# Attention of block 2 computed with channels as rows, its k times v moved into the written-out order

## The chip, the cores and the metric
One core of one Trainium2 chip runs the kernel. The metric is the device time of a run in microseconds (us), as the median of three runs. Engines are called PE (TensorE: matrix products), PEld (its weight loads), ACT (ScalarE), DVE (VectorE), POOL (GpSimd) and SP (SyncE, which here only issues DMAs).

## What is computed
Linear attention without softmax over 8 batches of 576 tokens with 8 heads of 64 channels, an RMS norm per head, and then two feed-forward layers over the 4608 tokens.

```python
kv = np.einsum('bhsd,bhse->bhde', k, v)
out = np.einsum('bhsd,bhde->bhse', q, kv)
rms = np.sqrt(np.mean(out * out, axis=-1, keepdims=True) + 1e-06)
x = (out / rms * g_norm)                       # as rows of 8 * 64 = 512
h = np.maximum(np.maximum(x @ w1, x @ w2), x @ w3)
y = h @ w_out                                  # 512 -> 768 -> 512
xn = y / np.sqrt(np.mean(y * y, -1, keepdims=True) + 1e-6) * rms_g
g = xn @ w_gate
result = (g * sigmoid(g) * (xn @ w_val)) @ w_out2   # 512 -> 1536 -> 512
```

## The kernel before
**Tiles and stages.** The 4608 tokens are cut in nine blocks of 512 (TB), counted 0 to 8. The activations of a block are kept with channels as rows, `X[t]`, as two tiles of fp32r whose sum is the value (a high and a low part). The ordinary product of the layers, mm3, is three fp32r products of 128x512 (high by high, high by low, low by high); twelve of them, four blocks of channels c, make one column block of a projection. P1.3.2 in the order below is such a group for block 1, column block 3, weight matrix 2. Plain fp32 products, which need no split, are used where operands are small.

**Attention.** For a batch b, kv_part(b, 0 to 4) multiplies k by v head by head: 40 products of 64x64 into one PSUM tile pk. kv_copy(b) takes pk out. From batch 2 on, kv_split writes the two parts of it to kvr: two ACT copies (L349), one for each half of the partitions, and two DVE subtractions (L351). Batches 0 to 2 are also copied by ACT (L366, L367) to kvbd, a matrix of 128x128 blocks on the diagonal, in fp32.
- Blocks 0 to 2 go token by token (128 tokens each, token_steps): po multiplies q by kvbd (L407), ACT squares, DVE sums over the heads, POOL takes the power -0.5, DVE scales (xn, L384), PE transposes (pt, L435), and ACT and DVE write the two parts of X.
- Blocks 3 to 8 go with channels as rows (wide_block): q and kv are both split and multiplied by mm3, ACT keeps the product and its square, DVE sums the squares in pieces, two products with the matrix fold (halves) complete the sums, POOL takes the power over 32 columns, and the factors are brought to their places through DRAM (spread, respread to the tile fr). The output then needs no transposes.

**What sets the order.** The kernel writes its own order; each engine runs its instructions as they come. Up to column block 3 of block 1 the string ORDER is read word by word: `ld:x` issues a load on SP, `P` a group of 12 products, `kv2.0` a part of k times v, `kc2` kv_copy, `s1`, `s2`, `h`, `hsI`, `hsL` the steps of the maximum and its split, and the letters A U X S H B I L the eight steps in which the weights, which come as 64-bit floats, are converted (A, H, B, L on DVE, U, X, S, I on ACT); Uo4 is step U for block 4 of w_out. After the string the rest runs in slots: `at(n, fn)` plans fn for the n-th next slot, and tick() runs the slot's functions between two groups of products. In do_p(t, j, mid) three groups of 12 follow each other with a slot between them.

**Buffers.** All weights, raw loads, q, kv and split tiles share one pool of 37 buffers of 4 KB per partition, up. A tile takes a buffer that is free or about to be, and its first writer then waits for the last user of the buffer. PSUM has two pools of four buffers.

In the kernel before, block 2 and batch 2 stand at the seam: its loads `ld:q4 ld:kv2` are issued late in ORDER, its k times v is in the first slot after ORDER (kv_do(0, 2)), its four tokens are planned at slots 1, 3, 5 and 7, and q block 5 is loaded in slot 2. `build_fold()` stands after ORDER.

```python
kv_do(0, 2)
for m in range(NS):
    token(1 + 2 * m, 2 * NS + m)
at(2, lambda: load_q(5))
at(3, lambda: new_x(2))
kv_load_at(6, 3)
kv_do(13, 3)
do_p(0, J1 - 1, pumped)
```

Of the kernel before, what the change touches and what calls it, by code (L numbers as in the profile page):

```python
# [20 lines left out]
P = 128  # L21
# [4 lines left out]
TB = 512  # L26
# [1 line left out]
NS = TB // P  # L28
KC = DM // P
NP = H // 2  # L30
WIDE = 3
WIDE_KV = WIDE * 512 // 576
J1, J2 = F1 // P, F2 // P
EPS = 1e-6
TOP = float(np.array(0x47F00000, dtype=np.uint32).view(np.float32))
# [15 lines left out]
hsL0.2 Bw32 Uo2 P1.1.0 Lw31 Iw32 Xo2 Lw32 So2 Ho2 P1.1.1 s11.1 Bo2 Io2 Lo2 P1.1.2 s21.1 ld:w50 P0.3.0 h1.1  # L51
hsI1.1 hsL1.1 Aw40 Uw40 ld:w51 P0.3.1 s10.3 Xw40 Sw40 Hw40 ld:w52 Aw41 Uw41 P0.3.2 Bw40 Xw41 s20.3 Iw40 Sw41
Lw40 ld:o4 Aw42 Uw42 Hw41 O0.2 Xw42 h0.3 Bw41 Sw42 hsI0.3 Hw42 Iw41 Ao3 hsL0.3 Bw42 Uo3 P1.2.0 Lw41 Iw42 Xo3
Lw42 So3 Ho3 P1.2.1 s11.2 Bo3 Io3 Lo3 P1.2.2 s21.2 ld:o5 P0.4.0 h1.2 hsI1.2 hsL1.2 Aw50 Uw50 P0.4.1 s10.4 Xw50
Sw50 Hw50 Aw51 Uw51 P0.4.2 Bw50 Xw51 s20.4 Iw50 Sw51 Lw50 Aw52 Uw52 Hw51 O0.3 Xw52 ld:q4 ld:kv2 h0.4 Bw51 Sw52
hsI0.4 Hw52 Iw51 Ao4 hsL0.4 Bw52 Uo4 P1.3.0 Lw51 Iw52 Xo4 Lw52 So4 Ho4 P1.3.1 s11.3 Bo4 Io4 Lo4 P1.3.2 s21.3
h1.3 hsI1.3 hsL1.3 Ao5 Uo5 Xo5 So5 Ho5 Bo5 Io5 Lo5
"""

# [2 lines left out]
def tile_kernel(ctx: ExitStack, tc, qT, k, v, kvt0, kvt1, w1, w2, w3, wo, wg, wv, wo2, out):  # L62
# [29 lines left out]
    def f32(ap):  # L92
        return ap.bitcast(F32)
# [260 lines left out]

    def kv_copy(b):
        pk = PK.pop(b)
        if b >= WIDE_KV:
            kv_split(pk, b)
        if b > WIDE_KV:
            del KV[b]  # L360
            kvbd.clear()
            kvb.clear()
            return
        m = kvb[b % 2]
        n = NP // 2 if b == 0 else NP
        nc.scalar.activation(m[:D, :n, 0:D], pk[:D, :n], AF.Copy)  # L366
        nc.scalar.activation(m[D:, :n, D:], pk[D:, :n], AF.Copy)  # L367
        if b == 0:
            pk = PK.pop("odd")
            nc.vector.tensor_copy(m[:D, n:, 0:D], pk[:D, n:])  # L370
            nc.vector.tensor_copy(m[D:, n:, D:], pk[D:, n:])
        kvbd[b] = m
        del KV[b]
# [77 lines left out]
    def cut_of(i):  # L451
        return slice(i % NS * P, (i % NS + 1) * P)

    def token(n, i):

        st = token_steps(i)
        for m, names in ((0, ("po", "sq")), (1, ("ss", "pw")), (3, ("xn",)), (4, ("pt", "hi")), (5, ("lo",))):
            for name in names:
                at(n + m, st[name])

    def wide_block(t, s):

        st = {}
        nb = TB // 32

        def split(m):
            if m == 0:
                st["y"] = xp.tile([P, KC, TB], F32, tag="x", name="y")
                st["hi"] = xp.tile([P, KC, TB], F32R, tag="x", name="qh")
                st["part"] = hp.tile([P, KC, nb], F32, tag="part", name="part")  # L470
            for c in range(2):
                nc.scalar.activation(st["hi"][:, 2 * m + c], Q[2 * t + m][:, c], AF.Copy)

        def rest(m):
            q = Q.pop(2 * t + m)
            lo = st["lo", m] = unit([P, 2, TB], F32R, "ql")
            for c in range(2):
                nc.vector.tensor_tensor(lo[:, c], q[:, c], f32(st["hi"][:, 2 * m + c]), ALU.subtract)

        def po(c):  # L480
            hi, lo = st["hi"][:, c], st["lo", c // 2][:, c % 2]
            o = psum([P, TB], "po")
            b = t * TB // S
            n = min(TB, (b + 1) * S - t * TB)
            for w, f in ((kvr[b], slice(0, n)), (kvr.get(b + 1), slice(n, TB))):
                if f.start < f.stop:
                    mm3(o[:, f], w[:, 0, c], w[:, 1, c], hi[:, f], lo[:, f], True, True)
            if c % 2:
                del st["lo", c // 2]
            if c + 1 == KC:  # L490
                del st["hi"]
            nc.scalar.activation(st["y"][:, c], o, AF.Copy)
            sq = st["sq", c] = tmp("sq")
            nc.scalar.activation(sq, o, AF.Square)

        def part(c):
            sq = st.pop(("sq", c)).rearrange("p (j b) -> p b j", b=nb)
            nc.vector.tensor_reduce(st["part"][:, c], sq, AX.X, ALU.add, apply_transpose=True)

        def halves():  # L500
            st["ss"] = psum([P, 2, nb], "hs")
            part = st["part"]
            for m in range(2):
                nc.tensor.matmul(st["ss"], fold[:, m], part[:, 2 * m:2 * m + 2], start=m == 0, stop=m == 1)

        def factor():
            rs = st["rs"] = hp.tile([P, 2, nb], F32, tag="rs", name="rs")
            nc.vector.tensor_scalar(rs, st["ss"], 1.0 / D, EPS, ALU.mult, ALU.add)
            flat = rs.rearrange("p q b -> p (q b)")
            nc.gpsimd.tensor_tensor(flat, flat, mhalf.to_broadcast([P, 2 * nb]), ALU.pow)  # L510

        def spread():
            nc.scalar.dma_start(hr_d[t].rearrange("q (r f) -> (q r) f", f=2 * nb), st["rs"].rearrange("p c b -> p (c b)"))

        def respread():
            for n in range(2):
                if n == 0:
                    st["f"] = xp.tile([P, KC, TB], F32, tag="x", name="fr")
                nc.scalar.dma_start(
                    st["f"][n * D:(n + 1) * D].rearrange("p c f -> p (c f)"), hr_d[t][n:n + 1].to_broadcast([D, KC * TB])  # L520
                )

        def xn(c):
            x = st["x", c] = tmp("xn")
            f = st["f"].rearrange("p (m c) f -> p m (c f)", m=2)[:, c // 2]
            f = f.rearrange("p (j c b) -> p c j b", c=2, b=nb)[:, c % 2]
            xv, yv = (a.rearrange("p (j b) -> p j b", b=nb) for a in (x, st["y"][:, c]))
            nc.vector.scalar_tensor_tensor(xv, yv, gc, f, ALU.mult, ALU.mult)

        def hi(c):  # L530
            if c == 0:
                new_x(t)
            nc.scalar.activation(X[t][0][:, c], st["x", c], AF.Copy)
# [376 lines left out]
    def at(n, fn):  # L910
        plan.setdefault(n_slot[0] + n, []).append(fn)
# [251 lines left out]
    with tc.manual_schedule():  # L1163
# [43 lines left out]
                nc.gpsimd.tensor_tensor(hs[:, 1], mx.pop((t, j)), f32(hs[:, 0]), ALU.subtract)  # L1207

        for word in ORDER.split():
            if word == "gc":  # L1210
                nc.scalar.activation(gcb, first_tail[0][:, DM:DM + 1 + KC], AF.Copy)
                continue
            m = re.match("[a-z]+|[A-Z]", word)
            kind, rest = m.group(), word[m.end():]
            if word.startswith("hs"):
                kind, rest = word[:3], word[3:]
            elif word[:2] in ("s1", "s2"):
                kind, rest = word[:2], word[2:]
            if kind in "AUXSHBIL":
                weight_step(kind, weight_key(rest))  # L1220
                continue
            if kind == "ld":
                load_word(rest[1:])
                continue
            n = [int(x) for x in rest.split(".")]
            if kind == "kv":
                kv_part(*n)
            elif kind == "kc":
                kv_copy(n[0])
            elif kind == "busy":  # L1230
                busy(n[0])
            elif kind == "P":
                up_word(*n)
            elif kind == "O":
                do_o(1, *n, J1)
            elif kind in ("s1", "s2", "h", "hsI", "hsL"):
                max_word(kind, *n)
            else:
                tok[n[0]][kind]()
        build_fold()  # L1240

        def pumped():
            tick()
# [5 lines left out]
        def kv_do(n, b):  # L1249
            at(n, lambda: do_kv(b))  # L1250

        kv_do(0, 2)
        for m in range(NS):
            token(1 + 2 * m, 2 * NS + m)
        at(2, lambda: load_q(5))
        at(3, lambda: new_x(2))
        kv_load_at = lambda n, b: at(n, lambda: load_kv(b))
        kv_load_at(6, 3)
        kv_do(13, 3)
# [8 lines left out]
        wait += [Prep(i, jp) for jp in range(J2 // 2) for i in range(3)]  # L1268
        for j in range(J1 - 1):
            if j in (1, 3):  # L1270
                load_q(2 * WIDE + j // 2)
            do_o(1, 1, j, J1)
            slot()

# [134 lines left out]
```

## Time and profile before

| | before |
|---|---|
| median of 3 runs | 1454.26 us (1454.23 to 1454.78) |
| the profiled execution | 1454.48 us, span in the trace 1452.7 us |
| PE busy | 1445.7 us of the span, 7106 products |
| DVE busy | 925.0 us |
| ACT busy | 637.6 us |
| POOL busy | 433.5 us |

A timeline gives start, duration, engine, line, operation, tiles, shapes and count, and in brackets how long the engine was idle before and what ended it. Products overlap: what one costs is the distance from its start to the next one's, not its duration. A plain fp32 product has two records on PE, so eight records of L407 are four products.

### The profile page before, as it was taken

What the parts mean: (1) busy time and instruction counts of PE and PEld (TensorE: products, weight loads), DVE (VectorE), ACT (ScalarE), POOL (GpSimd) and SP (SyncE); (2) the same over time, 40 slices, a digit from 0 to 9 for tenths busy, and PEclk for the clock granted to TensorE, in tenths of its full rate; (3) what the DMA queues carried; (4) which work ended last, traced back from release to release, by engine and by line L of the source; (5) the groups of instructions that cost most, each with busy time, mean ns of one, the idle gap of its engine ahead of it and who ended that gap; (6) DMA issues with size and microseconds to landing.
All of it is one profiled execution on the core that took longest, in us unless ns stands there. A gap on an engine that the chain in (4) does not pass through costs nothing.

```text
span 1452.7 us, 19796 instructions
## 1 busy us (share of the span) xinstructions
PE 1445.7 (100%) x7106; PEld 1204.4 (83%) x7106; DVE 925.0 (64%) x1401; ACT 637.6 (44%) x1136; POOL 433.5 (30%) x295
## 2 busy tenths in 40 slices
PE   9999999999999999999999999999999999999999
PEld 8888888888888888888888888888888888888887
DVE  6854477786768695962446475664675655754756
ACT  6863355454545564622224333343243442433422
POOL 3212231313131313121332252441334422532423
PEclk9999999999999999999999999999999999999999
DMA  9432357575757565769669464784666843784542
GB/s 366 156 94 81 95 182 268 189 259 186 281 194 261 188 248 184 275 251 393 232 217 349 158 248 187 284 302 183 231 243 252 329 175 132 297 310 175 192 177 102
DMA packets 109426, 324.13 MB, mean 223 GB/s; under 512 B 13264, under 2 KB 13520, under 8 KB 108560
## 3 DMA queue, kind: packets, MB, share of 16 engines
q1 hardware_dynamic: 95840, 296.14, 55.5%
q10 hardware_dynamic: 13488, 26.73, 5.8%
q8 instruction: 56, 0.92, 0.3%
q14 instruction: 42, 0.34, 0.1%
HBM read 249.30 MB, written 73.52 MB: 222 GB/s over the span
## 4 chain that ended last, share of the span: by engine, by line
PE 99%; DVE 0%; issue 0%; ACT 0%; POOL 0%; POOLq 0%
PE ua L922 18%; PE p L558 10%; PE p L559 10%; PE p L560 10%; PE ub L922 9%; PE da L922 9%; PE db L922 4%; PE uc L922 4%; PE acc L558 4%; PE acc L559 4%; PE acc L560 4%; PE dc L922 2%; PE pk L334 1%; PE pg L558 1%; PE pg L560 1%; PE pv L560 1%
## 5 line engine op out<-in xcount | busy, mean ns | idle before, releaser
L558 PE MATMUL p<-x,w 128*128 128x512 f32 (+1 forms) x656 | 255.9, 390 | 0.0
L560 PE MATMUL p<-x,w 128*128 128x512 f32 (+1 forms) x656 | 253.7, 387 | 0.0
L559 PE MATMUL p<-x,w 128*128 128x512 f32 (+1 forms) x656 | 253.7, 387 | 0.0
L922 PE MATMUL ua<-xo,w 128*128 128x512 f32 x864 | 213.4, 389 | 0.0
L922 PEld LDWEIGHTS ua<-xo,w 128*128 128x128 f32 x864 | 162.2, 188 | 33.7
L577 POOL TENSOR_TENSOR ho<-sl,ho 128x512 fp32r<-128x512 f32 x72 | 98.2, 1370 | 302.1 <-ACT ho L576 274.2
L577 POOL TENSOR_TENSOR hs<-h,hs 128x512 fp32r<-128x512 f32 x45 | 67.3, 1496 | 393.2 <-ACT hs L576 384.0
L577 POOL TENSOR_TENSOR ho<-t,ho 128x512 fp32r<-128x512 f32 x96 | 123.9, 1295 | 134.0 <-ACT ho L576 81.2
L922 PE MATMUL ub<-xo,w 128*128 128x512 f32 x576 | 146.1, 389 | 0.0
L560 PEld LDWEIGHTS p<-x,w 128*128 128x128 f32 x656 | 123.2, 188 | 25.2
L558 PEld LDWEIGHTS p<-x,w 128*128 128x128 f32 x656 | 123.3, 188 | 24.7
L559 PEld LDWEIGHTS p<-x,w 128*128 128x128 f32 x656 | 123.3, 188 | 24.0
L922 PEld LDWEIGHTS ub<-xo,w 128*128 128x128 f32 x576 | 108.1, 188 | 22.4
L1004 ACT ACTIVATE s<-ua 128x512 f32<-128x512 f32 x96 | 57.3, 597 | 138.6 <-PE ua L922 138.6
L922 PE MATMUL da<-ho,wd 128*128 128x512 f32 x432 | 105.7, 389 | 0.0
L576 ACT ACTIVATE ho<-t 128x512 fp32r<-128x512 f32 x96 | 59.4, 627 | 99.9 <-DVE t L753 98.9
L922 PEld LDWEIGHTS da<-ho,wd 128*128 128x128 f32 x432 | 81.1, 188 | 16.8
L576 ACT ACTIVATE hs<-h 128x512 fp32r<-128x512 f32 x45 | 28.4, 632 | 135.3 <-DVE h L593 126.8
L952 DVE TENSOR_TENSOR c<-uc,s 128x512 f32<-128x512 f32 x48 | 33.1, 690 | 83.8 <-PE uc L922 83.8
L558 PE MATMUL acc<-hs,w 128*128 128x512 f32 x216 | 85.1, 394 | 0.0
L560 PE MATMUL acc<-hs,w 128*128 128x512 f32 x216 | 84.3, 390 | 0.0
L559 PE MATMUL acc<-hs,w 128*128 128x512 f32 x216 | 84.0, 389 | 0.0
(173 smaller groups left out, 2692.7 us busy)
## 6 DMA issues: line engine op xcount, KB each, us to landing
w<-wd SPq DMA_DIRECT2D x180, 512.0 KB, 7.3
wd<-ws SPq DMA_DIRECT2D x72, 512.0 KB, 3.3
wd<-wd SPq DMA_DIRECT2D x72, 512.0 KB, 7.0
wq<-wd SPq DMA_DIRECT2D x72, 256.0 KB, 7.8
xo<-td SPq DMA_DIRECT2D x32, 512.0 KB, 9.4
q<-in_qT SPq DMA_DIRECT2D x18, 512.0 KB, 5.6
raw<-in_w SPq DMA_DIRECT2D x18, 512.0 KB, 10.3
raw<-in_wo SPq DMA_DIRECT2D x18, 512.0 KB, 6.2
```

Of the source, the lines that this page charges most:

```text
L334: nc.tensor.matmul(pk[h * D:(h + 1) * D, hp, :], kk, vv, start=(c == 0 and hp in ((0, NP // 2) if b == 0 else (0,))), stop=(c == 4), skip_ ...
L558: nc.tensor.matmul(o, ah, bh, start=first, stop=False)
L559: nc.tensor.matmul(o, ah, bl, start=False, stop=False)
L560: nc.tensor.matmul(o, al, bh, start=False, stop=last)
L576: nc.scalar.activation(hs[:, 0], h, AF.Copy)
L577: nc.gpsimd.tensor_tensor(hs[:, 1], h, f32(hs[:, 0]), ALU.subtract)
L922: nc.tensor.matmul(o, aa, bb, start=first and q == 0, stop=last and q == 2, skip_group_check=True)
L952: nc.vector.tensor_tensor(t, p, s, ALU.add)
L1004: nc.scalar.activation(t, p, AF.Copy)
```

## The change
Block 2 becomes the first wide block (WIDE is 2), with a chain of its own: no split of q and kv, but four plain fp32 products of q (as columns) with kvbd, cut at the border between batches 1 and 2 (plain); the sums, the power and the way through DRAM are those of the other wide blocks, with the three DMAs on SP's queue in place of ACT's. The loads of q blocks 4 and 5 and of batch 2 move ahead of P0.4.0, the fold copies ahead of P1.2.2, and batch 2's k times v, its copies and the start of the wide block (the word wide, which runs one slot) ahead of P1.3.2. The token steps of block 2 are gone.

```diff
-WIDE = 3
-WIDE_KV = WIDE * 512 // 576
+WIDE = 2
+SPLIT_KV = (WIDE + 1) * TB // S
...
-Lw42 So3 Ho3 P1.2.1 s11.2 Bo3 Io3 Lo3 P1.2.2 s21.2 ld:o5 P0.4.0 h1.2 hsI1.2 hsL1.2 Aw50 Uw50 P0.4.1 s10.4 Xw50
-Sw50 Hw50 Aw51 Uw51 P0.4.2 Bw50 Xw51 s20.4 Iw50 Sw51 Lw50 Aw52 Uw52 Hw51 O0.3 Xw52 ld:q4 ld:kv2 h0.4 Bw51 Sw52
-hsI0.4 Hw52 Iw51 Ao4 hsL0.4 Bw52 Uo4 P1.3.0 Lw51 Iw52 Xo4 Lw52 So4 Ho4 P1.3.1 s11.3 Bo4 Io4 Lo4 P1.3.2 s21.3
+Lw42 So3 Ho3 P1.2.1 s11.2 Bo3 Io3 Lo3 fold P1.2.2 s21.2 ld:o5 ld:q4 ld:q5 ld:kv2 P0.4.0 h1.2 hsI1.2 hsL1.2 Aw50 Uw50 P0.4.1 s10.4 Xw50
+Sw50 Hw50 Aw51 Uw51 P0.4.2 Bw50 Xw51 s20.4 Iw50 Sw51 Lw50 Aw52 Uw52 Hw51 O0.3 Xw52 h0.4 Bw51 Sw52
+hsI0.4 Hw52 Iw51 Ao4 hsL0.4 Bw52 Uo4 P1.3.0 Lw51 Iw52 Xo4 Lw52 So4 Ho4 P1.3.1 s11.3 Bo4 Io4 Lo4 kv2.0 kv2.1 kv2.2 kv2.3 kv2.4 kc2 wide P1.3.2 s21.3
...
+        first = t == WIDE
+        queue = nc.sync if first else nc.scalar
...
+        def plain(c):
+            if c == 0:
+                st["y"] = []
+                st["part"] = hp.tile([P, KC, nb], F32, tag="part", name="part")
+            if c % 2 == 0:
+                y = unit([P, 2, TB], F32, "y")
+                st["y"] += [y[:, 0], y[:, 1]]
+            q = Q[2 * t + c // 2][:, c % 2]
+            o = psum([P, TB], "po")
+            b = t * TB // S
+            n = min(TB, (b + 1) * S - t * TB)
+            nc.tensor.matmul(o[:, :n], kvbd[b][:, c, :], q[:, :n], start=True, stop=True)
+            if n < TB:
+                nc.tensor.matmul(o[:, n:], kvbd[b + 1][:, c, :], q[:, n:], start=True, stop=True)
+            if c % 2:
+                del Q[2 * t + c // 2]
+            keep(c, o)
...
+        if first:
+            for c in range(KC):
+                at(s + c // 2, lambda c=c: plain(c))
+                at(s + 1 + c // 2, lambda c=c: part(c))
+                at(s + 11 + c // 2, lambda c=c: xn(c))
+                at(s + 12 + c // 2, lambda c=c: hi(c))
+                at(s + 13 + c // 2, lambda c=c: lo(c))
+            for m, fn in ((4, halves), (5, factor), (7, spread), (7, respread)):
+                at(s + m, fn)
+            return
...
+            if word == "wide":
+                wide_block(WIDE, 0)
+                tick()
+                continue
+            if word == "fold":
+                build_fold()
+                continue
...
-        build_fold()
...
-        kv_do(0, 2)
-        for m in range(NS):
-            token(1 + 2 * m, 2 * NS + m)
-        at(2, lambda: load_q(5))
-        at(3, lambda: new_x(2))
```

PE around batch 2's k times v, before. The first row ends the first group of do_p(0, 5), the last rows begin its second; a name in brackets is a semaphore that the instruction waits for (DMAHW0 to 7 are those of the loads).

```order
L560 MATMUL p_1291<-x,w 128x512
L334 MATMUL pk<-kv 64x64 [waits DMAHW7_49,DMAHW2_49,Activation_49]
L334 MATMUL pk<-kv 64x64 x15
L334 MATMUL pk<-kv 64x64 [waits DMAHW3_49,DMAHW0_49]
L334 MATMUL pk<-kv 64x64 x7
L334 MATMUL pk<-kv 64x64 [waits DMAHW4_49,DMAHW1_49]
L334 MATMUL pk<-kv 64x64 x15
L558 MATMUL p_1355<-x,w 128x512 [waits DVE_49]
L559 MATMUL p_1355<-x,w 128x512
```

PE around the same products now. The row before them ends P1.3.1; L487 and L489 are the two products of plain for c=0 and c=1, and L585 begins P1.3.2 (L585 to L587 are mm3, L558 to L560 before).

```order
L587 MATMUL p<-x,w 128x512
L334 MATMUL pk<-kv 64x64 [waits DMAHW3_49,DMAHW0_49,DVE_49]
L334 MATMUL pk<-kv 64x64 x15
L334 MATMUL pk<-kv 64x64 [waits DMAHW4_49,DMAHW1_49]
L334 MATMUL pk<-kv 64x64 x7
L334 MATMUL pk<-kv 64x64 [waits DMAHW5_49,DMAHW2_49]
L334 MATMUL pk<-kv 64x64 x15
L487 MATMUL po<-q,kvbd 128x128 [waits DMAHW6_49,DVE_49]
L489 MATMUL po<-q,kvbd 128x384 [waits Activation_49]
L487 MATMUL po<-q,kvbd 128x128
L489 MATMUL po<-q,kvbd 128x384
L585 MATMUL p<-x,w 128x512 [waits PE_49]
```

The k times v has moved ahead of P1.3.2, and products with q stand directly behind it, the second of them with a wait for ACT.

ACT over the conversion of o4 and batch 2's copies, before. L138, L118, L140 and L150 are the steps U, X, S and I; the first row is Uo4, the second Iw52, the sixth Io4; L1197 is s11.3, L1204 hsI1.3, and after it come the same four steps for o5.

```order
L138 ACTIVATE wt<-raw 128x512 [waits DMAHW4_49,PE_49,Pool_49]
L150 ACTIVATE w<-wt 128x512 [waits DVE_49,Activation_49]
L118 ACTIVATE wt<-wt 128x512
L140 ACTIVATE wt<-wt 128x512 [waits Activation_49]
L1197 ACTIVATE s_1231<-p 128x512 [waits PE_49]
L150 ACTIVATE w<-wt 128x512 [waits DVE_49]
L1204 ACTIVATE hs<-h 128x512 [waits DVE_49]
...
L585 ACTIVATE s_1304<-p_1291 128x512
L349 ACTIVATE kvr<-pk 64x4x64 [waits DMAHW2_49,PE_49,Pool_49]
L349 ACTIVATE kvr<-pk 64x4x64
L366 ACTIVATE kvbd<-pk 64x4x64 [waits DVE_49]
L367 ACTIVATE kvbd<-pk 64x4x64
```

The same steps now, from Uo4 (the first row) to the copies of the first wide product; L1224 is s11.3.

```order
L138 ACTIVATE wt<-raw 128x512 [waits DMAHW4_49,DMAHW0_49,PE_49]
L150 ACTIVATE w<-wt 128x512 [waits DMAHW3_49,DVE_49]
L118 ACTIVATE wt<-wt 128x512 [waits Activation_49]
L140 ACTIVATE wt<-wt 128x512 [waits Activation_49]
L1224 ACTIVATE s_1257<-p 128x512
L150 ACTIVATE w<-wt 128x512 [waits DMAHW1_49,DMAHW4_49,DVE_49,PE_49]
L349 ACTIVATE kvr<-pk 64x4x64 [waits PE_49,Pool_49]
L349 ACTIVATE kvr<-pk 64x4x64
L366 ACTIVATE kvbd<-pk 64x4x64 [waits DVE_49]
L367 ACTIVATE kvbd<-pk 64x4x64
L509 ACTIVATE y<-po 128x512 [waits PE_49]
L511 ACTIVATE sq<-po 128x512
```

The split and the copies of batch 2 have moved directly behind Io4, and Uo4 has DMAHW0 and another place of PE in its wait.

## Rows read from the trace of the kernel before
**Rows 1.** The page: busy time by engine, granted clock by slice, shares of the chain
```profile
PE 1445.7 (100%) x7106; PEld 1204.4 (83%) x7106; DVE 925.0 (64%) x1401; ACT 637.6 (44%) x1136; POOL 433.5 (30%) x295
...
PEclk9999999999999999999999999999999999999999
...
PE 99%; DVE 0%; issue 0%; ACT 0%; POOL 0%; POOLq 0%
```

**Rows 2.** Timeline of PE, 118 to 125 us: start, duration, what
```profile
118.46 2.55 PE L334 MATMUL pk<-kv 128*64 128x64 f32 x80
120.94 0.50 PE L558 MATMUL p<-x,w 128*128 128x512 f32 x1
121.27 0.39 PE L559 MATMUL p<-x,w 128*128 128x512 f32 x1
121.50 0.40 PE L560 MATMUL p<-x,w 128*128 128x512 f32 x1
...
123.79 1.05 PE L407 MATMUL po<-kvbd,q 128*128 128x128 f32 x8
124.60 0.48 PE L558 MATMUL p<-x,w 128*128 128x512 f32 x1
124.92 0.40 PE L559 MATMUL p<-x,w 128*128 128x512 f32 x1
```

**Rows 3.** Timeline of PE: transposes ahead of L407, and ahead of ordinary products
```profile
141.93 0.60 PE L435 MATMUL pt<-ident,xn 128*128 128x128 f32 x4
142.37 1.06 PE L407 MATMUL po<-kvbd,q 128*128 128x128 f32 x8
...
161.72 0.60 PE L435 MATMUL pt<-ident,xn 128*128 128x128 f32 x4
162.08 0.48 PE L558 MATMUL acc<-hs,w 128*128 128x512 f32 x1
```

**Rows 4.** Timeline of PE: the halves of block 3
```profile
192.52 0.53 PE L504 MATMUL hs<-part,fold 128*128 128x32 f32 x4
192.88 0.48 PE L558 MATMUL acc<-hs,w 128*128 128x512 f32 x1
193.20 0.39 PE L559 MATMUL acc<-hs,w 128*128 128x512 f32 x1
```

**Rows 5.** Timeline of ACT: Uo4, So4, s11.3 and Io4
```profile
107.73 0.67 ACT L138 ACTIVATE wt<-raw 128x512 int32<-128x512 uint32 x1 [0.48 <-issue]
...
110.43 0.63 ACT L140 ACTIVATE wt<-wt 128x512 f32<-128x512 f32 x1
110.97 0.58 ACT L1197 ACTIVATE s<-p 128x512 f32<-128x512 f32 x1
112.28 0.63 ACT L150 ACTIVATE w<-wt 128x512 fp32r<-128x512 f32 x1 [0.73 <-DVE wt L146]
```

**Rows 6.** Timeline of DVE: Lo4
```profile
112.94 0.69 DVE L152 TENSOR_TENSOR w<-wt,w 128x512 fp32r<-128x512 f32 x1 [0.70 <-ACT w L150]
```

**Rows 7.** Timeline of ACT: split and copies of batch 2
```profile
121.52 0.75 ACT L349 ACTIVATE kvr<-pk 64x256 fp32r<-64x256 f32 x2
125.14 0.38 ACT L366 ACTIVATE kvbd<-pk 64x256 f32<-64x256 f32 x1 [2.86 <-DVE kvr L351]
125.53 0.38 ACT L367 ACTIVATE kvbd<-pk 64x256 f32<-64x256 f32 x1
```

**Rows 8.** Timeline of DVE: low parts of batch 2's split
```profile
124.24 0.86 DVE L351 TENSOR_TENSOR kvr<-pk,kvr 64x256 fp32r<-64x256 f32 x2
```

**Rows 9.** Timeline of PE at the start: warming products
```profile
1.36 5.49 PE L307 MATMUL busy<-ident 128*128 128x128 f32 x24 [1.36 <-POOL ident masks.py:199]
...
8.05 2.05 PE L307 MATMUL busy<-ident 128*128 128x128 f32 x16
```

**Rows 10.** Power of the wide blocks (ns min/median/max); DMA issues with median us to landing
```profile
L510 POOL TENSOR_TENSOR rs<-rs,mhalf x6: 5556/5728/6031, 196.8 to 556.2; 128x32 f32<-128x32 f32 x6
...
fr<-hr ACTq DMA_DIRECT2D x12, 512.0 KB, 6.3
```

More of the change, by code (lines that the diff above doesn't have):

```diff
@@ L356, in kv_copy @@
         pk = PK.pop(b)
-        if b >= WIDE_KV:
+        if b >= SPLIT_KV:
             kv_split(pk, b)
-        if b > WIDE_KV:
+        if b > SPLIT_KV:
             del KV[b]
@@ L452, in cut_of @@
         return slice(i % NS * P, (i % NS + 1) * P)
[L454 to L459, printed above, removed]
     def wide_block(t, s):
@@ L464, in wide_block @@
         nb = TB // 32
+        first = t == WIDE
+        queue = nc.sync if first else nc.scalar
         def split(m):
             if m == 0:
-                st["y"] = xp.tile([P, KC, TB], F32, tag="x", name="y")
+                y = xp.tile([P, KC, TB], F32, tag="x", name="y")
+                st["y"] = [y[:, c] for c in range(KC)]
                 st["hi"] = xp.tile([P, KC, TB], F32R, tag="x", name="qh")
@@ L491, in po, with keep @@
                 del st["hi"]
-            nc.scalar.activation(st["y"][:, c], o, AF.Copy)
+            keep(c, o)
+        def keep(c, o):
+            nc.scalar.activation(st["y"][c], o, AF.Copy)
             sq = st["sq", c] = tmp("sq")
@@ L512, in spread @@
         def spread():
-            nc.scalar.dma_start(hr_d[t].rearrange("q (r f) -> (q r) f", f=2 * nb), st["rs"].rearrange("p c b -> p (c b)"))
+            queue.dma_start(hr_d[t].rearrange("q (r f) -> (q r) f", f=2 * nb), st["rs"].rearrange("p c b -> p (c b)"))
         def respread():
@@ L518, in respread @@
                     st["f"] = xp.tile([P, KC, TB], F32, tag="x", name="fr")
-                nc.scalar.dma_start(
+                queue.dma_start(
                     st["f"][n * D:(n + 1) * D].rearrange("p c f -> p (c f)"), hr_d[t][n:n + 1].to_broadcast([D, KC * TB])
@@ L526, in xn @@
             f = f.rearrange("p (j c b) -> p c j b", c=2, b=nb)[:, c % 2]
-            xv, yv = (a.rearrange("p (j b) -> p j b", b=nb) for a in (x, st["y"][:, c]))
+            xv, yv = (a.rearrange("p (j b) -> p j b", b=nb) for a in (x, st["y"][c]))
             nc.vector.scalar_tensor_tensor(xv, yv, gc, f, ALU.mult, ALU.mult)
@@ L1270, in tile_kernel @@
             if j in (1, 3):
-                load_q(2 * WIDE + j // 2)
+                load_q(2 * WIDE + 2 + j // 2)
             do_o(1, 1, j, J1)
```

## The prediction
> **What bounds the kernel now.** I read the head of the page first: TensorE (PE) is busy for 1445.7 of 1452.7 us, and the chain that ended last is 99% PE [rows 1]. So whatever PE no longer issues comes off the end, and whatever PE newly waits for is put on it; the other engines count only where PE waits for them. The profiled execution took 1454.48 us, 0.2 more than the median of 1454.26; the terms below are differences, and I set them on the median.
>
> **What PE gets rid of, and what it gets.** PE's timeline shows prices as distances between starts. Ordinary 128x512 products follow each other every 0.23 us; the second product after a block of plain fp32 ones starts 0.32 to 0.33 after the first, so a change back costs 0.09 to 0.10 [rows 2].
> - Removed: four token steps of q times kv (L407). One is 8 records, from 123.79 to 124.60, 0.81 us, and 0.09 for the change back: 4 x 0.90 = 3.60 [rows 2].
> - Removed: four groups of transposes (L435). One that stands right ahead of an L407 block costs 0.44 (141.93 to 142.37) with no change back of its own, one ahead of ordinary products 0.36 and 0.09 [rows 3]. I take 0.44 for each of the four: 1.76.
> - Added: four plain fp32 products of 512 columns, each cut in two at column 128. That is the same number of columns as in four L407 blocks. At L407's price per column they cost 4 x 0.81 = 3.24; the bound from above is four passes, each at the 0.23 of an ordinary product: 4 x 4 x 0.23 = 3.7. I take 3.24, since L407 is the same kind of product. They come in two groups, and the first follows k times v directly, whose change back (0.10) it shares: one change more, 0.09, so 3.33.
> - Added: the two products that sum the squares (halves). Their twins at L504 take 0.36 and 0.09 for the change back [rows 4]: 0.45.
> - k times v of batch 2 only moves: 2.48 us before and after [rows 2].
>
> The sum for PE is -5.36 + 3.33 + 0.45 = **-1.58 us**, and -1.1 with the dearer bound. That is all that the change can gain.
>
> **Where the new place makes PE wait.** In the order of before, batch 2's k times v is followed by 12 ordinary products and then by a token that still reads batch 1; the first product with the new matrix comes after four such groups of 12 (12 x 0.227 = 2.72 us each) and that token. In the changed order the word wide issues its first two products at once: kv, kc2, c=0 on 128 columns of batch 1, and then c=0 on 384 columns with the matrix that kc2 has just begun to write. PE takes its work in order, so P1.3.2 and everything behind it is queued behind that wait. The row of L489 names ACT as what it waits for: the copies L366 and L367. L366 in turn waits for DVE's L351, in the order of before as well.
>
> How late is that copy? On ACT, ahead of the split and the copies, stands the conversion of the weight o4, from Uo4 to Io4. In the order of before Uo4 ran at 107.73, beside P1.3.0 [rows 5]. In the changed one its row waits for DMAHW0, on which the first k load of batch 2 lands, and for PE: by the value in the built program, for the 16th of batch 2's 40 products. The pool of 37 buffers is that short once two q blocks and five kv buffers are loaded ahead: the working buffer of o4 is one that batch 2's rows leave. So a conversion that used to run beside products begins only when batch 2's own products run. Let t0 be the start of the first of these:
> - 16 of 40 products are issued at 0.4 x 2.48 = 0.99, and I allow 0.25 for the last one to end and be seen (an estimate): Uo4 starts at t0 + 1.25.
> - From Uo4 to the start of Io4 the trace has the same instructions in the same order: 107.73 to 112.28, 4.55 us [rows 5]. Io4 starts at t0 + 5.80.
> - L349 follows on ACT 0.54 later, the distance at which ACT starts work that waits for nothing (110.43 to 110.97), and takes 0.75 for its two halves [rows 5, 7]: t0 + 7.1. On DVE, Lo4 starts 0.66 after Io4 does (112.94) and is nearly through by then [rows 6].
> - A handover takes 0.03 there (112.28 + 0.63 to 112.94); L351 on DVE takes 0.86 [rows 6, 8]: t0 + 8.0. L366 and L367 take 0.77 [rows 7]: t0 + 8.8, and PE goes on at about t0 + 8.85.
> - Without the wait PE would be there at t0 + 2.48 + 0.2 = t0 + 2.68.
>
> The stall is **6.2 us**, with bounds half a microsecond to either side for the six handovers of the chain. Nothing hides it, as PE takes no work past it. The sum is -1.58 + 6.2 = **+4.6 us**.
>
> **What the clock may add.** The granted clock is at its upper level (2.4 GHz) in every slice of the page [rows 1]. But the first 24 warming products take 5.49 us, 0.229 each, and 16 later ones 2.05, 0.128 each [rows 9]: after it had done nothing PE worked at about half speed for 5.5 us, a loss of 24 x 0.10 = 2.4 us, or of 3.1 against the 0.101 of L407's records. After the start PE is never idle for long, so no row tells what 6 us of idleness do. The bounds are 0 and 3.1. I take 2.0, as the start is the only row of a PE that comes out of idleness. The Trainium skill (TensorE: Matmul & The Clock Gate, Part 1: The HAM clock gate) says that half the clock is the state of an idle engine, lifted by activity and brought back by idling. The start agrees with the first half of that; no run here shows the second. By that rule the loss is there; without it the sum is the +4.6.
>
> **What costs nothing.** The chain of block 2 is longer now: a power over 32 columns (5.7 us on POOL), a store and two loads through DRAM [rows 10]. From the halves, ahead of the last third of do_p(1, 4), to do_p(2, 0) PE has ten groups of 12 products and batch 3's 2.48: 29.7 us. The chain takes 2.8 until DVE sees the sum, 5.7, for the little store no more than the 6.3 of the loads fr, 6.3 for fr, and about 2.5 for xn, hi and lo: 23.6. It fits; if that cover were gone, PE would wait at do_p(2, 0) for the rest of the chain. Batch 3's six loads now stand behind these transfers on SP's queue: they go out by some 18 us after the halves and are needed at 27.2; with a flight like fr's they have 3 us to spare. ACT has four copies more and DVE four reductions instead of eight small steps, on engines that PE does not wait for there. The eight loads of q and kv that go out earlier have more time than before. The 24 fold copies move on DVE to a place ahead of s21.2; the PSUM pool has four buffers, so PE needs the one that s21.2 frees only some groups of products later.
>
> **The rivals.**
> - *The stall alone, at the full clock.* For it: the page shows the upper level everywhere, even where the start was slow. Against it: that start. 1454.3 + 4.6 = 1458.9.
> - *The conversion is not held up*, that is, Uo4 begins by t0 - 2.6 and only split and copies are waited for: 0.13 from the end of k times v, then 0.75, 0.86, 0.77 and three handovers of 0.05, some 2.7, less the 0.2 of the first 128 columns: a stall of 2.5, and 2.5 - 1.58 = +0.9, or 1455.2: not slower by what can be measured. It decides from a stall of under 4.5. Against it: Uo4's wait in the built program.
> - *SP's queue holds batch 3's loads too long*, on top of the forecast: with twice fr's flight PE waits at batch 3's products for 18 + 12.6 - 27.2 = 3.4 us: 1464.3. Against it: the 3 us to spare.
> - *A gain*: only if PE finds the matrix written within 1.58 us; at most those 1.58, half of what can be told from no change.
>
> **How the numbers follow.** Stall and half clock: 0.48, 1454.3 + 4.6 + 2.0 = **1460.9**. Stall alone: 0.37. No hold-up: 0.08. Queue: 0.05. Anything else: 0.02. The range takes in the first two with their bounds, from 1454.3 + 5.7 - 1.58 = 1458.4, less 0.4 for the scatter of the runs, to 1454.3 + 6.7 - 1.58 + 2.75 (the middle of the clock's two upper bounds) = 1462.2. A measurement of this kernel tells 0.2%, 2.9 us, from no change: above 1457.2 is slower. Slower 0.88, same 0.10, faster 0.02.
>
> **What would show it.** A row of L489 on PE with 6 us of idleness ahead of it, released by ACT's L367; Uo4 on ACT a little over 1 us after the first of batch 2's products; ordinary products 0.45 apart just after, if the clock fell; no wait ahead of do_p(2, 0) and of batch 3's products. The prediction is wrong if L489 starts within 3 us of the end of k times v, or if PE waits at a second place.

## The result, and the profile after

| | before | after |
|---|---|---|
| median | 1454.52 us (4 runs, 1454.23 to 1454.89) | 1462.40 us (4 runs, 1461.58 to 1463.56) |
| the profiled execution | 1454.48, span 1452.7 | 1462.26, span 1460.4 |
| PE records | 7106 | 7078 |
| mean granted clock | 0.999 | 0.998 |

The ratio is 1.0055, with a 95% interval of 1.0037 to 1.0072: the changed kernel is 7.9 us slower. The direction and most of the size are those of the forecast (1460.9), but the median lies 0.2 us above the range (1458.0 to 1462.2). The kernel before has a median of 1454.52 with its fourth run; the forecast started from 1454.26.

The page of after, beside [rows 1]. PE has fewer instructions and yet is busy for longer; its share of the chain that ended last is 97% in place of 99%.

```profile
PE 1447.1 (99%) x7078; PEld 1203.4 (82%) x7078; DVE 926.9 (63%) x1398; ACT 638.9 (44%) x1140; POOL 432.6 (30%) x292
...
PEclk9999999999999999999999999999999999999999
...
PE 97%; issue 1%; DVE 1%; POOL 0%; ACT 0%; POOLq 0%; DVEq 0%
```

The list of PE's waits in after: engine, tile and line, what is waited for, us in total, times, the longest. The two rows shown are new; the three between them stand in the list of before as well.

```profile
PE po L489 <- ACT kvbd L367: 6.0, 1, 6.0
...
PE db L949 <- POOL ho L604: 0.4, 1, 0.4
```

PE's timeline around the new place, beside [rows 2]: batch 2's k times v, the first products of the wide block, the ordinary products behind them, and (last two rows) the start of L489 and of the third L585 when the same sequence comes again some 9 us later.

```profile
112.96 2.55 PE L334 MATMUL pk<-kv 128*64 128x64 f32 x80
115.44 0.49 PE L487 MATMUL po<-q,kvbd 128*128 128x128 f32 x2
121.91 1.65 PE L489 MATMUL po<-q,kvbd 128*128 128x384 f32 x2 [5.97 <-ACT kvbd L367]
...
124.48 1.20 PE L585 MATMUL p<-x,w 128*128 128x512 f32 x1
125.48 0.63 PE L586 MATMUL p<-x,w 128*128 128x512 f32 x1
125.91 0.63 PE L587 MATMUL p<-x,w 128*128 128x512 f32 x1
...
127.15 0.39 PE L585 MATMUL p<-x,w 128*128 128x512 f32 x1
...
131.45 0.81 PE L489 MATMUL po<-q,kvbd 128*128 128x384 f32 x2
...
134.35 0.40 PE L585 MATMUL p<-x,w 128*128 128x512 f32 x1
```

Two things are to be seen. First, L489 could have started at 115.64 (0.2 behind L487) and starts at 121.91: **6.27 us** of stall, ended by ACT's copy L367. Second, what follows is slow. From L489 to the third L585 the sequence takes 5.24 us (121.91 to 127.15), and the second time 2.90 (131.45 to 134.35): **2.34 us** lost at a place where PE waits for nothing. The granted clock by stretch names the reason (columns: stretch, its length, busy us of PE, PEld, DVE, ACT, POOL, granted clock, DMA share, GB/s):

```profile
116.00:119.00 3.00, 0.00 (x0) 0.00 (x0) 1.70 (x3) 2.19 (x5) 0.00 (x0) 1.00 0.00 0
119.00:122.00 3.00, 0.10 (x1) 0.10 (x1) 2.23 (x4) 1.47 (x5) 0.00 (x0) 0.63 0.01 3
122.00:125.00 3.00, 3.00 (x7) 1.83 (x7) 0.00 (x0) 1.08 (x2) 0.00 (x0) 0.50 0.00 0
125.00:128.00 3.00, 3.00 (x11) 2.41 (x10) 0.00 (x0) 1.08 (x2) 0.00 (x0) 0.74 0.00 0
```

The clock falls to its lower level (1.2 GHz) while PE is idle, stays there through 122 to 125, when PE works again, and comes back to 2.4 GHz between 125 and 128. That is also why PE's busy time grew: the same products last longer. The page's row PEclk, whose slices are 36 us long, shows nothing of this.

ACT's and DVE's timelines of after over the stall, beside [rows 5 to 8] (L138 is Uo4, L150 at 118.44 Io4):

```profile
114.16 0.70 ACT L138 ACTIVATE wt<-raw 128x512 int32<-128x512 uint32 x1 [3.27 <-PE pk L334]
...
118.44 0.63 ACT L150 ACTIVATE w<-wt 128x512 fp32r<-128x512 f32 x1 [0.78 <-issue]
118.98 0.75 ACT L349 ACTIVATE kvr<-pk 64x256 fp32r<-64x256 f32 x2
...
120.19 0.86 DVE L351 TENSOR_TENSOR kvr<-pk,kvr 64x256 fp32r<-64x256 f32 x2 [0.39 <-issue]
121.08 0.38 ACT L366 ACTIVATE kvbd<-pk 64x256 f32<-64x256 f32 x1 [1.35 <-DVE kvr L351]
121.47 0.38 ACT L367 ACTIVATE kvbd<-pk 64x256 f32<-64x256 f32 x1
```

Uo4 waits on PE's L334, so the conversion of o4 starts 1.20 us behind the first of batch 2's products. Everything up to L367 is the chain that the prediction wrote down. (Uw52, the U step of the weight ahead of it, is late as well: 107.68 here, 104.03 before. PE does not wait for that.)

**Where the rest is.** To compare the kernels I cut each profiled execution in three: up to the first projection product, from there to the halves of block 3 (L504 before, L521 after), and the rest. The first cut falls at 25.17 before and at 25.11 to 25.73 in the other kernels (25.11 in after): the head of the kernel waits for the k and v loads, and its scatter is not the change's. The stretch between the cuts holds all that the change touches. It takes 167.35 us before (25.17 to 192.52) and 174.39 in after (25.11 to 199.50), 7.04 more. The rest, up to the execution's own time, takes 1261.96 (1454.48 - 192.52) and 1262.76 (1462.26 - 199.50), 0.80 more. The last row of PE's waits belongs to that rest.

### The profile page after: what moved, and what is told of

The parts are those of the page before. It is cut to its first block, busy times and chain, and to the rows that moved or that the text cites. A ratio compares the mean times of both kernels' runs of the same rounds, so it can differ in the third digit from the quotient of the medians.

```text
span 1460.4 us, 19758 instructions
## 1 busy us (share of the span) xinstructions
PE 1447.1 (99%) x7078; PEld 1203.4 (82%) x7078; DVE 926.9 (63%) x1398; ACT 638.9 (44%) x1140; POOL 432.6 (30%) x292
## 4 chain that ended last, share of the span: by engine, by line
PE 97%; issue 1%; DVE 1%; POOL 0%; ACT 0%; POOLq 0%; DVEq 0%
PE ua L949 17%; PE p L585 10%; PE p L587 10%; PE p L586 10%; PE da L949 9%; PE ub L949 9%; PE db L949 4%; PE uc L949 4%; PE acc L585 4%; PE acc L586 4%; PE acc L587 4%; PE dc L949 2%; PE pk L334 1%; PE pg L585 1%; PE pv L585 1%
## 5 line engine op out<-in xcount | busy, mean ns | idle before, releaser
L585 PE MATMUL p<-x,w 128*128 128x512 f32 (+1 forms) x656 | 256.9, 392 | 0.0
L587 PE MATMUL p<-x,w 128*128 128x512 f32 (+1 forms) x656 | 254.1, 387 | 0.0
L949 PE MATMUL ua<-xo,w 128*128 128x512 f32 x864 | 213.4, 389 | 0.0
L949 PEld LDWEIGHTS ua<-xo,w 128*128 128x128 f32 x864 | 162.2, 188 | 33.7
L604 POOL TENSOR_TENSOR ho<-sl,ho 128x512 fp32r<-128x512 f32 x72 | 98.0, 1368 | 302.3 <-ACT ho L603 290.4
L604 POOL TENSOR_TENSOR hs<-h,hs 128x512 fp32r<-128x512 f32 x45 | 66.7, 1482 | 397.3 <-ACT hs L603 339.4
L604 POOL TENSOR_TENSOR ho<-t,ho 128x512 fp32r<-128x512 f32 x96 | 124.2, 1298 | 133.7 <-ACT ho L603 82.4
L949 PE MATMUL ub<-xo,w 128*128 128x512 f32 x576 | 146.2, 389 | 0.0
L585 PEld LDWEIGHTS p<-x,w 128*128 128x128 f32 x656 | 123.5, 188 | 25.2 <-issue 0.3
L587 PEld LDWEIGHTS p<-x,w 128*128 128x128 f32 x656 | 123.3, 188 | 25.4
L949 PEld LDWEIGHTS ub<-xo,w 128*128 128x128 f32 x576 | 108.1, 188 | 22.4
L949 PE MATMUL da<-ho,wd 128*128 128x512 f32 x432 | 105.7, 389 | 0.0
L949 PEld LDWEIGHTS da<-ho,wd 128*128 128x128 f32 x432 | 81.1, 188 | 16.8
L585 PE MATMUL acc<-hs,w 128*128 128x512 f32 x216 | 85.0, 394 | 0.0
L616 DVE TENSOR_TENSOR s<-p,s 128x512 f32<-128x512 f32 x45 | 31.0, 689 | 84.2 <-PE p L587 68.7
L587 PE MATMUL acc<-hs,w 128*128 128x512 f32 x216 | 84.3, 390 | 0.0
```

Source lines behind the costliest of these rows:

```text
L585: nc.tensor.matmul(o, ah, bh, start=first, stop=False)
L587: nc.tensor.matmul(o, al, bh, start=False, stop=last)
L604: nc.gpsimd.tensor_tensor(hs[:, 1], h, f32(hs[:, 0]), ALU.subtract)
L616: nc.vector.tensor_tensor(s2, p, s1, ALU.max)
L949: nc.tensor.matmul(o, aa, bb, start=first and q == 0, stop=last and q == 2, skip_group_check=True)
```

## The experiments

The kernel before ran beside the experiments in two groups: 1454.44 us (21 runs) beside "products in the stall", "the q load", "the copies" and "k times v one group earlier", 1454.40 (17 runs) beside the other three. The times after each experiment are medians.

### Products in the stall
```diff
+            if c == 0:
+                for _ in range(24):
+                    nc.tensor.matmul(o[:, n:n + P], ident, ident, start=True, stop=True)
             nc.tensor.matmul(o[:, :n], kvbd[b][:, c, :], q[:, :n], start=True, stop=True)
```


> 24 plain fp32 products of the identity with itself are put ahead of the first wide product, into its own PSUM tile and overwritten by it; everything else is the changed kernel. They take 24 x 0.20 = 4.9 us of PE inside the 6.3 us wait, so the wait for the copy ends at the same time, but PE is idle for only some 1.3 us. Theory (the time is PE's -1.6, the stall of 6.3, and 2.3 for a clock that fell because PE idled): granted clock 1.0 after the wait, ordinary products 0.23 apart at once, 2.3 us less than the changed kernel: about 1460.1, or 1459.4 without the 0.7 that its profiled execution lost at its very end. Rival (the slow stretch after the wait belongs to the new products or to the first use of what ACT wrote, not to idleness): 1462.4 and the slow stretch still there.

1460.31 us (1459.61 to 1460.68, 4 runs), 1.0041 of before [1.0027, 1.0054]: 2.1 us less than after, with 24 products more. PE's timeline (L489 are the added products, L492 is the product that waits, L588 the ordinary one):

```profile
113.57 2.55 PE L334 MATMUL pk<-kv 128*64 128x64 f32 x80
116.05 5.62 PE L489 MATMUL po<-ident 128*128 128x128 f32 x48
121.51 0.39 PE L490 MATMUL po<-q,kvbd 128*128 128x128 f32 x2
122.53 0.91 PE L492 MATMUL po<-q,kvbd 128*128 128x384 f32 x2 [0.63 <-ACT kvbd L367]
...
123.85 0.69 PE L588 MATMUL p<-x,w 128*128 128x512 f32 x1
...
125.53 0.39 PE L588 MATMUL p<-x,w 128*128 128x512 f32 x1
```

The granted clock is 1.00 in every stretch from 113 to 128 us, and from L492 to the third ordinary triple the sequence takes 3.00 us (122.53 to 125.53), 0.10 more than the 2.90 of the undisturbed one. L492 itself starts as long after the end of k times v as in after: the products fill the stall and don't shorten it. So the slow stretch in after is a cost of its own, it follows from PE's idleness, and it is worth a little over 2 us of the 7.9.

### The q load behind k times v
```diff
-... ld:o5 ld:q4 ld:q5 ld:kv2 P0.4.0 ...
+... ld:o5 ld:q4 ld:kv2 P0.4.0 ...
-... Lo4 kv2.0 kv2.1 kv2.2 kv2.3 kv2.4 kc2 wide P1.3.2 s21.3
+... Lo4 kv2.0 kv2.1 kv2.2 kv2.3 kv2.4 ld:q5 kc2 wide P1.3.2 s21.3
```


> Only the load of q block 5 moves, from ahead of P0.4.0 to just behind batch 2's k times v, so one of the 37 buffers fewer is taken when o4 is converted. Theory (the conversion of o4 is held up by a buffer that batch 2's rows occupy): Uo4 on ACT is back beside P1.3.0, about 5 us ahead of the first of batch 2's products, the wait of L489 falls from 6.0 to about 2.6, and the time to 1454.5 - 1.6 + 2.6 = 1455.5 if the clock stays, 1457.8 if 2.6 us of idleness are enough for it to fall. Rival (the wait is split and copies alone, and o4's place does not matter): the wait stays at 6.0 and the time at 1462.4.

1457.10 us (1455.45 to 1458.31, 10 runs), 1.0020 [1.0011, 1.0030]. One buffer less is taken ahead, and o4's conversion runs where it ran before. ACT's timeline, then PE's with one row of DVE's:

```profile
107.77 0.68 ACT L138 ACTIVATE wt<-raw 128x512 int32<-128x512 uint32 x1 [0.48 <-issue]
...
115.69 0.77 ACT L349 ACTIVATE kvr<-pk 64x256 fp32r<-64x256 f32 x2 [2.76 <-PE pk L334]
```

```profile
115.53 0.49 PE L487 MATMUL po<-q,kvbd 128*128 128x128 f32 x2
118.26 0.91 PE L489 MATMUL po<-q,kvbd 128*128 128x384 f32 x2 [2.25 <-ACT kvbd L367]
...
177.59 1.41 DVE L728 SCALAR_TENSOR_TENSOR y<-y,gcb,rb 128x512 f32<-128x512 f32 x2 [3.92 <-DMA rb<-rs]
...
180.71 0.36 PE L586 MATMUL po<-ql,kvr 128*128 128x192 f32 x1 [0.86 <-DVE ql L474]
```

The wait falls from 5.97 to 2.25 us. So 3.7 us of the long stall come from the early load: with it, Uo4 waits for PE's reads of batch 2's rows; without it, Uo4 does not wait. What is left is k times v, split, copies, the prediction's second rival (a stall of 2.5). The clock stays at 1.00. The time is 1.6 above what was expected. The last row explains over half of that: PE waits 0.86 us in block 3 for a low part of q (ql). DVE writes it late, because it stands idle for 3.92 us ahead of L728 until the transfer rb lands (2.21 us in "k times v one group earlier", where q block 5 is loaded as late and PE has no such wait). So this wait does not follow from the late load alone; why the transfer lands late here was not tried.

### The copies ahead of the split
```diff
         pk = PK.pop(b)
-        if b >= SPLIT_KV:
-            kv_split(pk, b)
         if b > SPLIT_KV:
+            kv_split(pk, b)
...
         kvbd[b] = m
+        if b == SPLIT_KV:
+            kv_split(pk, b)
```


> In kc2 the two ACT copies to kvbd stand ahead of the split (L349, L351) and not behind it; buffers and order are else those of the changed kernel. Theory: the chain is shorter by L349's 0.75 and L351's 0.86, the wait of L489 falls from 6.0 to about 4.3, and the time to 1454.5 - 1.6 + 4.6 = 1457.5 with the clock up, 1459.8 if 4.3 us of idleness still bring it down (which of the two is open; it places the border between 2.6 and 6). Rival (the wait is the conversion of o4 alone): the wait stays at 6.0, 1462.4.

1459.66 us (1458.98 to 1460.00, 4 runs), 1.0036 [1.0023, 1.0050], close to the 1459.8 that was expected with a fallen clock. PE waits 3.85 us (expected: 4.3). PE's timeline, and the granted clock in the stretches around it (columns as above):

```profile
120.25 1.17 PE L490 MATMUL po<-q,kvbd 128*128 128x384 f32 x2 [3.85 <-ACT kvbd L366]
...
124.90 0.40 PE L586 MATMUL p<-x,w 128*128 128x512 f32 x1
```

```profile
120.00:120.50 0.50, 0.25 (x1) 0.26 (x2) 0.26 (x1) 0.47 (x2) 0.00 (x0) 1.00 0.00 0
120.50:121.00 0.50, 0.50 (x2) 0.27 (x2) 0.00 (x0) 0.47 (x2) 0.00 (x0) 0.77 0.00 0
...
122.00:125.00 3.00, 3.00 (x9) 1.94 (x8) 1.00 (x2) 1.62 (x4) 0.00 (x0) 0.64 0.01 3
```

The split was 2.1 us of the stall; the conversion ahead of it, unchanged, keeps the rest. The clock still falls, here half a microsecond after PE has gone on, and the sequence from L490 takes 4.65 us in place of 2.90: 1.75 lost.

### The wide block behind the next group
```diff
-... kv2.4 kc2 wide P1.3.2 s21.3
+... kv2.4 kc2 P1.3.2 wide s21.3
```


> The wide block is issued behind the 12 products of the third projection group of block 3 (one slot later in the written order) instead of ahead of them; nothing else is moved. They take 12 x 0.23 = 2.7 us. Theory (ScalarE's copies come at a time that TensorE does not set): the wait shrinks from 6.0 to about 3.3 us, since the copies stay where they are and 2.7 us of work now lie ahead of it. Whether the clock falls in a wait of 3.3 us the runs so far do not say: it stayed at 1.00 through 2.25 us and fell behind 3.85 us. If it falls the time is about 1454.5 + 3.5 - 1.6 + 2.2 + 0.7 = 1459.3; if it stays, 1457.1. Rival (the copies wait for the wide block's place in the order, not for time): the wait stays at 6.0 us and the time at 1462.

1458.79 us (1458.25 to 1459.67, 6 runs), 1.0031 [1.0020, 1.0042]. PE's timeline, and the granted clock:

```profile
118.85 0.38 PE L487 MATMUL po<-q,kvbd 128*128 128x128 f32 x2
122.47 1.65 PE L489 MATMUL po<-q,kvbd 128*128 128x384 f32 x2 [3.24 <-ACT kvbd L367]
```

```profile
122.20:122.40 0.20, 0.00 (x0) 0.00 (x0) 0.14 (x1) 0.20 (x1) 0.00 (x0) 0.57 0.00 0
...
122.00:125.00 3.00, 2.53 (x6) 1.60 (x6) 1.36 (x3) 1.25 (x4) 0.00 (x0) 0.54 0.00 0
```

The copies end where they did, 2.7 us of work lie ahead of them, and the wait is 3.24. The clock falls to its lower level just ahead of PE's return at 122.47, and the sequence from L489 loses 1.65 us. The kernel is 4.4 us slower than before: the first of the two cases that were written down (1459.3), less the 0.7 us at the end of the kernel, which are absent here.

### k times v one group earlier
```diff
-... So4 Ho4 P1.3.1 s11.3 Bo4 Io4 Lo4 kv2.0 kv2.1 kv2.2 kv2.3 kv2.4 kc2 wide P1.3.2 s21.3
+... So4 Ho4 kv2.0 kv2.1 kv2.2 kv2.3 kv2.4 s11.3 kc2 ld:q5 P1.3.1 Bo4 Io4 Lo4 wide P1.3.2 s21.3
```
(`ld:q5` is also gone from its early place.)

> Batch 2's k times v and kc2 stand a group earlier, between P1.3.0 and P1.3.1 (kc2 behind s11.3 and ahead of Io4), and q block 5 is loaded behind them; the wide block starts where it does in the changed kernel. Theory: no wait of PE for L367 and no slow stretch, PE's saving is all that is left: 1454.5 - 1.6 = 1452.9, and within 0.5 of it. Rival (the wide block costs by itself, by its chain through DRAM, its three transfers on SP's queue or its products): 1455 or more, with a wait of PE later than 130 us.

1453.77 us (1453.29 to 1454.93, 11 runs), 0.9996 [0.9987, 1.0005]. PE's timeline of the place:

```profile
110.39 2.55 PE L334 MATMUL pk<-kv 128*64 128x64 f32 x80
...
115.72 0.38 PE L487 MATMUL po<-q,kvbd 128*128 128x128 f32 x2
115.94 0.81 PE L489 MATMUL po<-q,kvbd 128*128 128x384 f32 x2
```

Split and copies run beside P1.3.1 and are through at 115.56; L489 has no wait. From the first projection to block 3's halves this kernel takes 165.95 us (25.27 to 191.22), **1.40 less** than before. That is the change's saving with nothing set against it. The median is 0.9 us above the 1452.9 that was expected, so that value was missed; the profiled execution (1453.29) is within the 0.5. No time this small can be told from no change. The edit moves the q load as well as k times v, so it does not say which of the two is needed; "the q load behind k times v" and "the wide block behind the next group" do. With the late load alone PE waits 2.25 us, with a group of products between and the early load 3.24; here, with both, it does not wait.

### k times v in its old place
```diff
+        at(0, lambda: load_q(5))
+        kv_do(0, 2)
+        wide_block(WIDE, 1)
...
-                at(s + 11 + c // 2, lambda c=c: xn(c))
+                at(s + 9 + c // 2, lambda c=c: xn(c))
...
-            for m, fn in ((4, halves), (5, factor), (7, spread), (7, respread)):
+            for m, fn in ((3, halves), (4, factor), (6, spread), (6, respread)):
```
(the words `kv2`, `kc2`, `wide` and `ld:q5` leave ORDER, and `ld:q4 ld:kv2` stand where they stood before.)

> Batch 2's products kv2 stay where the kernel before has them, behind the whole of block 3's projections, with the shape of the change's wide block one slot behind them, and block 2's chain moved forward by as much as fits (its folds two slots ahead of the changed kernel's). Theory (the shorter work on TensorE is worth 1.6 us by itself, and all of the loss comes from the place of the 40 products in the written order): no wait for the copies above 1 us, the clock at 1.00, and 1454.5 - 1.6 = 1452.9 us, 0.9989 of before. Rival (the wide block itself costs, wherever it stands, since its fp32 products or its chain hold up others): 1454.5 or more.

1453.33 us (1452.88 to 1454.96, 10 runs), 0.9994 [0.9984, 1.0003]. The list of PE's waits has no row for kvbd's copies in the wide block, the clock is at 1.00, and the stretch to block 3's halves takes 166.13 us (25.63 to 191.76), 1.22 less than before. So neither the wide block nor its longer chain holds up anything that can be measured; the new order does. This edit puts the loads back too, so it doesn't tell their share from that of the 40 products. It is the fastest of all kernels run here, though not by what can be told from no change.

### The changed kernel again


> The changed kernel once more, unchanged, to see what of its excess of 7.9 us over the kernel before is always there. Theory (the stall at the wide block, with the clock's loss behind it): TensorE's first product of the wide block again waits about 6.0 us for ScalarE's copy of kvbd, the 16 products behind it again take 4.4 us where 2.2 would do, and the time is again 1461.6 to 1463.6 us. Open is the 0.4 us for which TensorE waits at the end of the kernel for GpSimd (db behind ho): if it belongs to the change it recurs; if it is scatter it is absent here, and the time is then nearer 1461.9.

1462.30 us (1460.74 to 1462.95, 5 runs), 1.0053 [1.0041, 1.0066]. The wait for L367 is 5.97 again; the sequence behind it takes 5.40 us (122.48 to 127.88), 2.50 lost where the first profile had 2.34. The wait of 0.4 us at L949 recurs too, so it is no scatter of a single execution.

### All together

| kernel | wait of PE at the wide block | granted clock, lowest 3 us | lost behind it | to block 3's halves, against before | the rest, against before | median |
|---|---|---|---|---|---|---|
| after | 5.97 | 0.50 | 2.34 | +7.04 | +0.80 | 1462.40 |
| after, again | 5.97 | 0.50 | 2.50 | +7.20 | +0.76 | 1462.30 |
| products in the stall | 0.63 (and 5.46 of products) | 1.00 | 0.10 | +4.80 | +0.84 | 1460.31 |
| copies first | 3.85 | 0.64 | 1.75 | +4.36 | +0.76 | 1459.66 |
| wide one group later | 3.24 | 0.54 | 1.65 | +3.66 | +0.10 | 1458.79 |
| q load late | 2.25 | 1.00 | 0.12 | +2.18 | +0.13 | 1457.10 |
| k times v earlier | none | 1.00 | | -1.40 | +0.11 | 1453.77 |
| k times v in its old place | none | 1.00 | | -1.22 | +0.13 | 1453.33 |

The columns between are each worked out as for after: from the starts of L489 (L490, L492 where lines shifted) and of the third ordinary triple behind it, less 2.90; and from the two cuts. The third column is the lowest of the stretches from 113 to 128 us.

## Why the prediction was right in its mechanism, and short in its sum

- **PE is the bound, and takes no work past a wait: right.** What an experiment took away of the stall and of the slow stretch came off the time to block 3's halves, within 0.3 us.
- **The stall of 6.2 us and its cause: right.** Measured 6.27. Uo4 starts at t0 + 1.20 (said: 1.25), Io4 at t0 + 5.48 (said: 5.80), PE goes on at t0 + 8.95 (said: 8.85). That the size fits to 0.1 is partly luck: up to Io4 the chain is 0.32 shorter than said, behind it 0.42 longer, since L351 starts 0.46 behind the end of L349 (118.98 + 0.75 to 120.19) where 0.03 was taken. That a buffer caused it is shown by the late q load, which alone brings Uo4 back to 107.77 and the wait to 2.25.
- **PE's own work, -1.58: right.** In after, 7.04 less the stall (6.27) and the clock's loss (2.34) leaves -1.57; in after again, 7.20 - 6.26 - 2.50 leaves -1.56. The kernel with k times v earlier saves 1.40, with one change of product kind more than after: the 12 products behind k times v take 2.85 us there (112.87 to 115.72), not 12 x 0.227 = 2.72.
- **No second wait, and nothing set down for the rest: the step that failed most.** PE waits neither at do_p(2, 0) nor at batch 3's products, and SP's queue holds nothing back. Yet the rest of the kernel behind block 3 takes 0.8 us more, and most of it is lost around the wait at L949. The prediction gave "anything else" a chance of 0.02 and no price. By its own sign it is wrong there: PE waits at a second place.
- **The clock, 2.0 with bounds 0 and 3.1: the step that failed in its size.** The mechanism was right. That idleness in the middle of the kernel brings the lower level is what no row of before could show; after waits of 3.24 us and more these runs do. But it cost 2.34 and 2.50 in the two profiles, not 2.0. The Trainium skill (TensorE: Matmul & The Clock Gate, Part 1: The HAM clock gate) has an idle engine fall back to half the clock. The traces agree for these waits; after the one of 2.25 us the clock stayed up.
- **The range.** The stall alone was wrong as a rival (the clock did fall). With the measured terms the sum is 6.27 - 1.57 + 2.34 + 0.80 = 7.8, where the forecast had 6.6 and the medians differ by 7.9. The upper end of the range took the middle of the clock's two upper bounds and left nothing for later waits and for the scatter: the nine runs of the changed kernel reach from 1460.74 to 1463.56, the 17 runs of before beside the last group of experiments from 1453.51 to 1455.02. An end of 1462.9 would have followed from the clock's full bound (1454.3 + 6.7 - 1.58 + 3.1) and the 0.4 of scatter that the lower end was given, and would have held the result. The start from 1454.26 and not 1454.52 is as large as the miss.

## The 0.8 us at the end

The timelines of DVE and POOL show what is different there. Before (ACT's rows left out; L577 is POOL's split of ho):

```profile
1429.15 1.30 POOL L577 TENSOR_TENSOR ho<-t,ho 128x512 fp32r<-128x512 f32 x1 [2.09 <-ACT ho L576]
1429.34 1.65 DVE L999 TENSOR_TENSOR sl<-c,sl 128x512 f32<-128x512 f32 x1
```

After, the same place (L604 is L577's line there, L1026 that of L999), with PE's rows:

```profile
1436.54 0.69 DVE L1026 TENSOR_TENSOR sl<-c,sl 128x512 f32<-128x512 f32 x1
1436.65 1.72 POOL L604 TENSOR_TENSOR ho<-t,ho 128x512 fp32r<-128x512 f32 x1 [2.09 <-ACT ho L603]
1436.94 1.07 PE L949 MATMUL db<-ho,wd 128*128 128x512 f32 x4
...
1438.42 0.73 PE L949 MATMUL db<-ho,wd 128*128 128x512 f32 x2 [0.41 <-POOL ho L604]
...
1438.99 1.53 PE L949 MATMUL ua<-xo,wq 128*128 128x512 f32 x6
```

By distances between starts the six products db take 2.05 us (1436.94 to 1438.99), against 1.38 before (1429.78 to 1431.16): 0.67 of the 0.80. Another 0.1 is there in every kernel with the wide block, also in those without this wait (column "the rest" above).

Where a DVE and a POOL instruction of this kind overlap (all inputs in SBUF, none a product's result in PSUM), the one that starts second is the longer one in the pairs shown here. Before, POOL is 0.19 us ahead: it takes 1.30, and DVE, which has time, takes 1.65 in place of 0.69. In after DVE is 0.11 ahead, and it is POOL that takes 1.72; PE waits for its result.

What turns the order round can be seen 11 us earlier. POOL's split of ho is released there by the end of DVE's L1026, and L780 comes next on DVE, so both start at about the same time. First after, then "the wide block behind the next group":

```profile
1425.96 1.29 POOL L604 TENSOR_TENSOR ho<-t,ho 128x512 fp32r<-128x512 f32 x1 [1.23 <-DVE sl L1026]
1425.98 1.82 DVE L780 TENSOR_TENSOR t<-sl,t 128x512 f32<-128x512 f32 x1
```

```profile
1423.15 1.85 POOL L604 TENSOR_TENSOR ho<-t,ho 128x512 fp32r<-128x512 f32 x1 [1.25 <-DVE sl L1026]
1423.15 0.69 DVE L780 TENSOR_TENSOR t<-sl,t 128x512 f32<-128x512 f32 x1
```

In all four profiles with the wait POOL is 0.02 us ahead at this pair and DVE is the longer one. In the two where both start together (the second pair above, and k times v earlier) POOL is the longer one, and in the other three POOL is 0.37 us or more ahead; none of these five has the wait. Counted from block 3's halves, DVE's starts in the two kernels shown agree within 0.2 us over the 900 us ahead of the pair. So a tie within 0.02 us goes before the wait. In the profiles with the wait the stretch to block 3's halves is 4.4 us or more longer than before, in those without it 3.7 or less; whether that decides the tie was not tried and stays open.

## What to carry to other kernels

A load that is issued earlier takes a buffer earlier; look for the instruction that gets its buffer last, and ask what stands behind it on its engine: here a weight conversion with no part in the change held up the copies that PE waited for. An idle PE can cost more than its idleness, as the products behind it run at the lower clock: here the waits of 3.24 us and more were worth their own length and 1.7 to 2.5 us on top, the one of 2.25 us only 0.1. Work that follows its producer at once on the bounding engine needs other products between them and a producer that is not held up: the same change with its k times v one group earlier and its last q load behind it lost nothing, while a late load alone, or a group of products between alone, left a wait.

## What the hardware showed

- After waits of 3.24, 3.85 and 5.97 us the granted clock fell to its lower level and 1.65, 1.75 and 2.34 to 2.50 us were lost behind the wait; after 2.25 us it stayed at its upper level. In the waits of 5.97 and 3.24 us it fell while PE was idle, behind the one of 3.85 us when PE had worked for half a microsecond again.
- 24 plain fp32 products of 128x128, of no use to the result, made the kernel 2.1 us faster than the idleness that they filled.
- A POOL subtraction of 128x512 took 1.72 us in place of 1.30 where a DVE instruction of 0.69 with both inputs in SBUF had started 0.11 us ahead of it, and such a DVE instruction took 1.65 in place of 0.69 behind a POOL one. A DVE instruction with a product's result as an input did not lengthen it: behind DVE's c<-ub,s (1433.13 in after) POOL took 1.29.
